# Retention and a rational feed-forward on one core: the order of work made by a queue model, attention taken ahead, weights split with two integer operations

## The chip, the cores and the metric

The kernel runs on one core of a Trainium2 chip. The time is device microseconds of one execution, from launch to end; the median of several is given. The engines are TensorE (PE, matrix products; PEld is its weight load), VectorE (DVE), ScalarE (ACT), GpSimd (POOL) and SyncE (SP, which issues all the transfers here). They run side by side, each through its own instructions in a fixed order, and wait for one another by semaphores.

## The reference

```python
def _attn_ref(q, k, v):                       # 8 batches, 8 heads, 576 positions, 64 wide
    scores = 1/sqrt(64) * q @ k.T
    gamma = 1 - 2.0 ** (-5 - arange(H))
    ret = scores * where(rel >= 0, gamma ** rel, 0)     # rel = query position - key position
    return ret @ v

def _moe_ref(x, w_in, w_out, a, b):           # x 4608 x 512, w_in 512 x 2048, w_out 2048 x 512
    h = x @ w_in
    P = a[0] + a[1]*h + a[2]*h**2 + a[3]*h**3
    Q = 1 + |b[0]|*|h| + |b[1]|*h**2
    return (P / (Q + 1e-6)) @ w_out
```

The attention's output, heads side by side, is x. The weights arrive as 64-bit floats.

## The kernel before, in words

**Attention** goes in 36 chunks of 128 positions (4.5 a batch, so a chunk can hold the end of one batch and the start of the next). A chunk n is loaded as two tiles, qk and kv. `scale_q` multiplies q by a table on POOL; `scale_v` scales v head by head, eight operations on ACT; `scores` is 16 small products into a tile `ps` in PSUM; `decay` has POOL zero two corners of a tile `s` and DVE multiply the scores by masks into it, in three operations; `outputs` forms the chunk's own part, the state's increment and the part that comes from the running state `S_sb`. `keep_hi` (ACT) and `keep_lo` (DVE) split the result into two fp32r tiles xhi and xlo, `add` (DVE) and `fade` (POOL) carry the state on.

**Feed-forward** goes in nine blocks b of 512 tokens, and in each over 16 slices f of 128 hidden columns. A pair (b, f) is a *step*; there are 144, numbered in the order in which they run: block 0's first eight slices, block 1, block 0's other eight, then blocks 2 to 8. `gemm1` forms h in one PSUM bank with 12 products (three for each of four parts: high by high, high by low, low by high), `gemm2` adds g times w_out into the accumulators `acc` with another 12. Between them h becomes g in eleven element operations on 128x512 tiles: p (ACT, then two on DVE), u = |h| (ACT), a line in u (ACT, called v), v (DVE), Ln and Exp (ACT) for 1/Q, then three on DVE, the first of which joins P and 1/Q and the other two of which are a correction step, then the high part of g (ACT) and its low part (POOL in the first 24 steps, DVE later).

**Weights**: 32 tiles (w_in and w_out, 16 each) of 64-bit words. `split_weight` takes the upper words through ACT (`c`), then three integer operations on DVE (a shift, a join with the top bits of the lower words, the sign), then a high part (ACT) and a low part (POOL), both fp32r. Chunks 2 to 5 are loaded into the slots of weight tiles that arrive later.

**Order.** It is written by hand. `BEFORE`, `FIRST`, `DENSE`, `REST` and `END` are lists of names; for each step `run` calls the functions named there in that order, and every operation keeps that order on its engine (`InOrder`). Five chunks run before step 0, chunk 5 to 7 in steps 1, 3 and 5, the others by `SCORES`. The products of w_out follow by `lag` steps:

```python
def lag(i):
    return 4 if NF // 2 <= i < first - 4 or i >= len(steps) - 8 else 3
```

PSUM has eight banks: two for h, four for acc (two tiles), two for ps. The loads stand in SP's queue as `load_unit` and `load_weight` are called.

Of the kernel before, what the change touches and what calls it, by code (L numbers as in the profile page):

```python
# [12 lines left out]
F32 = mybir.dt.float32  # L13
# [3 lines left out]
I64 = mybir.dt.int64  # L17
AF = mybir.ActivationFunctionType
# [14 lines left out]
BEFORE = "split1 start scale_q scale_v scores decay outputs split2 add fade keep_hi keep_lo split3 split0".split()  # L33
FIRST = (
    "split1 gemm1 outputs ffn_p split2 ffn_hi keep_hi ffn_lo gemm2 ffn_r scale_q split3 add fade keep_lo start ffn_p2"
    " scale_v scores decay split0 ffn_q ffn_v"
).split()
DENSE = (
    "gemm1 outputs keep_hi split1 add fade keep_lo ffn_p split2 split0 ffn_v scale_q ffn_hi ffn_r ffn_lo scale_v gemm2"
    " ffn_p2 scores decay split3 ffn_q"  # L40
).split()
REST = (
    "gemm1 ffn_p outputs keep_hi add fade keep_lo ffn_hi ffn_p2 ffn_lo scores decay scale_q scale_v ffn_v gemm2 ffn_r ffn_q"
).split()
END = "ffn_r ffn_hi gemm2 ffn_lo ffn_q".split()

STARTS_BEFORE = [0, 1, 1, 2, 2]
STARTS = [1, 1, 2, 1, 2] + [1] * 19

SCORES = [1, 3, 5, 23, 25, 27, 29, *range(2 * NF, (NB - 1) * NF, 4)]  # L50
WARM = [8, 3, 2]
LN_SHIFT = 60
# [12 lines left out]

@with_exitstack
def retention_ffn(ctx: ExitStack, tc: tile.TileContext, qkv, w_in, w_out, ab, masks, gq, gv, out):

# [15 lines left out]
    cnv = ctx.enter_context(tc.tile_pool(name="cnv", bufs=4))  # L84
# [36 lines left out]
    def warm(n):
        for _ in range(n):
            pe.matmul(unread[:, 0, 0:P], zeros, zeros, start=True, stop=True)

    warm(WARM[0])
    a0, a1, a2, a3 = (ab_sb[:, i : i + 1] for i in range(4))
    b0, b1 = absb[:, 0:1], absb[:, 1:2]
    lnb = const.tile([P, 2], F32, name="lnb")
    QC = float(np.float32(1.0) + np.float32(1e-6))
    dve.memset(lnb[:, 0:1], math.ldexp(QC, -LN_SHIFT))  # L130
    dve.memset(lnb[:, 1:2], -LN_SHIFT * math.log(2.0))


    bits = {}
    parts = {}

    def load_weight(k):

        bits[k] = wts.tile([P, DM], I64, tag=f"w{k[0]}_{k[1]}", name=f"bits{k[0]}_{k[1]}")
        nc.sync.dma_start(bits[k], (w_in, w_out)[k[0]][k[1]])  # L140

    def split_weight(k):


        nm = f"{k[0]}_{k[1]}"
        words = bits[k].bitcast(I32).rearrange("p (c w) -> p c w", w=2)
        low, high = words[:, :, 0], words[:, :, 1]
        c = cnv.tile([P, DM], I32, tag="c", name=f"c{nm}")
        cf = c.bitcast(F32)


        act.activation(cf, high.bitcast(F32), AF.Abs, scale=math.ldexp(1.0, -112))
        yield
        dve.tensor_scalar(c, c, 3, 1, ALU.logical_shift_left, ALU.bitwise_or)
        yield
        dve.scalar_tensor_tensor(c, low, 29, c, ALU.logical_shift_right, ALU.bitwise_or)
        yield
        dve.scalar_tensor_tensor(c, high, -0x80000000, c, ALU.bitwise_and, ALU.bitwise_or)
        yield
        w = wts.tile([P, 2, DM], F32R, tag=f"w{nm}", name=f"w{nm}")  # L160
        del bits[k]
        act.activation(w[:, 0, :], cf, AF.Copy)
        pool.tensor_tensor(w[:, 1, :], cf, w[:, 0, :].bitcast(F32), ALU.subtract)
        parts[k] = w


    xs = {}
    st_a = {}
    scr = {}
# [9 lines left out]
    def scale_q(n):  # L179

        q = raws[n][0][:, 0]
        pool.tensor_tensor(q, q, gq_sb, ALU.mult)

    def scale_v(n):

        v = raws[n][1][:, 1]
        for h in range(H):
            act.activation(v[:, h], v[:, h], AF.Copy, scale=gv_sb[:, h : h + 1])

    def scores(n):  # L190


        q, k = raws[n][0][:, 0], raws[n][0][:, 1]
        by_acc = n < NP and n % 3 < 2
        ps = (ps_acc if by_acc else ps_at).tile([P, 2, 512], F32, tag="acc" if by_acc else "at", name=f"ps{n}")
        for c in range(2):
            for e in range(2):
                for t in range(2):
                    for j in range(2):

                        g, r, i0 = 2 * c + e, slice(j * D, j * D + D), 64 * (t == e)
                        pe.matmul(
                            ps[t * D : (t + 1) * D, j, g * P + i0 : (g + 1) * P],
                            k[r, g, t * D : (t + 1) * D], q[r, g, i0:], start=True, stop=True,
                        )
        st_a[n] = ps

    def decay(n):

        ret = scr[n] = gp.tile([P, 2, 2, 2, P], F32, tag="g", name=f"s{n}")  # L210
        out_ = ret.rearrange("p j c e i -> p (j c) e i")
        in_ = st_a[n].rearrange("p j (c e i) -> p (j c) e i", c=2, e=2)
        r = [slice(P - D, P), slice(0, D)]
        for e in range(2):
            pool.memset(out_[r[1 - e], :, e, 0:D], 0.0)
        i0 = int(n % 9 == 4)
        m = mask_sb[:, 1 + i0 : 4 + i0 : 2].unsqueeze(1).broadcast_to([P, 4, 2, D])
        dve.tensor_tensor(out_[:, :, :, D:], in_[:, :, :, D:], m, ALU.mult)
        for e in range(2):
            m = mask_sb[r[e], 2 * e].unsqueeze(1).broadcast_to([D, 4, D])  # L220
            dve.tensor_tensor(out_[r[e], :, e, 0:D], in_[r[e], :, e, 0:D], m, ALU.mult)

    def parts_of(n):

        ps = st_a[n]
        return (
            ps[:, :, 0:256].rearrange("p j (c i) -> p j c i", c=2),
            ps[:, :, 256:384].rearrange("p e (c d) -> p c e d", c=2),  # L230
        )

    def outputs(n):


        u = n % 9
        o, ds = parts_of(n)
        ret = scr.pop(n)
        q = raws[n][0][:, 0]
        k, v = (raws[n][1][:, a] for a in range(2))  # L240
        for j in range(2):
            for c in range(2):
                for t in range(2):
# [14 lines left out]
        if u != 0:  # L258
# [297 lines left out]
```

## Time and profile before

| | |
|---|---|
| median of the runs | 984.15 us (983.35 to 984.31, three runs) |
| span of the profiled execution, first to last instruction | 979.8 us (its own time is given by its span alone) |
| busy: PE, DVE, ACT, POOL | 922.1, 841.8, 712.4, 167.8 us |
| mean granted clock of PE | 0.985 |
| bytes moved | 65.44 MB, 54.96 MB of them read |

The profile is one execution. The busy time of an engine is the union of its instructions; register, semaphore and transfer-issuing instructions are not counted. In the views by line nearly all instructions have line 63, that of the helper that records every operation, so the groups are told apart by what they write and read: `h<-xhi,w` is a product of gemm1, `acc<-w,g` one of gemm2, `ps<-...` one of attention, `c<-bits,c` a step of splitting a weight. A row of such a group gives its count, then its busy time in us, the mean ns of one, and the idle time of the engine just before, with what ended it.

### The profile page before, as it was taken

How to read it: one execution, taken by the hardware profiler on the slowest of the kernel's cores; microseconds unless marked ns; L12 is line 12 of the kernel's file. 1: busy time of each engine (PE TensorE's matmuls, PEld its weight loads, DVE VectorE, ACT ScalarE, POOL GpSimd, SP SyncE). 2: the span in 40 equal slices, each digit the busy share in tenths (PEclk: the TensorE clock that was granted, in tenths of full speed). 3: DMA queues.
4: the chain of work that ended last, by engine and by line, in shares of the span. 5: the costliest groups of instructions: out<-in, count | busy, mean ns of one | idle time of the engine just before them, and what ended most of it. 6: DMA issues, size and time to landing. Idle time of an engine off the chain costs nothing.

```text
span 979.8 us, 16128 instructions
## 1 busy us (share of the span) xinstructions
PE 922.1 (94%) x6234; PEld 745.3 (76%) x6234; DVE 841.8 (86%) x1261; ACT 712.4 (73%) x1274; POOL 167.8 (17%) x200
## 2 busy tenths in 40 slices
PE   6768877888999999999999999999999999999997
PEld 6547765656788888888888888888888888888886
DVE  4999989998788988888888888888888888888895
ACT  5487777776776777877787777777777777767775
POOL 3554434344011111101111111101111111100000
PEclk8799999999999999999999999999999999999999
DMA  9945000002212111210121112110211121001001
GB/s 348 407 165 210 7 0 1 1 1 87 86 44 86 44 44 43 87 65 22 44 87 43 44 44 86 44 65 23 87 44 43 44 87 44 2 1 43 1 0 44
DMA packets 20557, 65.44 MB, mean 67 GB/s; under 512 B 2304, under 2 KB 2432, under 8 KB 20480
## 3 DMA queue, kind: packets, MB, share of 16 engines
q1 hardware_dynamic: 20480, 64.41, 18.2%
q8 instruction: 49, 0.80, 0.3%
q14 instruction: 28, 0.23, 0.1%
HBM read 54.96 MB, written 9.44 MB: 66 GB/s over the span
## 4 chain that ended last, share of the span: by engine, by line
PE 75%; DVE 15%; ACT 4%; issue 3%; DMA 1%; POOL 0%; SPq 0%; ACTq 0%; POOLq 0%
PE acc L63 35%; PE h L63 33%; PE ps L63 8%; DVE c L63 7%; DVE p L63 5%; DVE v L63 2%; ACT c L63 1%; DMA kv<-in_qkv 1%; DVE s L63 1%; ACT kv L63 1%; ACT u L63 1%; DMA qk<-in_qkv 0%; ACT o L63 0%; ACT w L63 0%; ACT v L63 0%
## 5 line engine op out<-in xcount | busy, mean ns | idle before, releaser
L63 PE MATMUL acc<-w,g 128*128 128x512 f32 x1632 | 401.0, 394 | 7.5 <-ACT o L63 4.0
L63 PE MATMUL h<-xhi,w 128*128 128x512 f32 x1152 | 382.0, 393 | 16.3 <-DVE p L63 14.7
L63 PEld LDWEIGHTS acc<-w,g 128*128 128x128 f32 x1632 | 301.5, 188 | 78.6 <-ACT o L63 4.9
L63 PEld LDWEIGHTS h<-xhi,w 128*128 128x128 f32 x1152 | 217.2, 189 | 66.6 <-DVE p L63 18.9
L63 PE MATMUL h<-xlo,w 128*128 128x512 f32 x576 | 225.3, 391 | 0.2 <-DVE xlo L63 0.2
L63 ACT ACTIVATE p<-h,ab_sb 128x512 f32<-128x512 f32 x144 | 111.2, 772 | 106.5 <-PE h L63 106.4
L63 ACT ACTIVATE u<-h 128x512 f32<-128x512 f32 x144 | 85.7, 595 | 76.0 <-DVE v L63 74.6
L63 DVE SCALAR_TENSOR_TENSOR p<-p,ab_sb,u 128x512 f32<-128x512 f32 x144 | 107.8, 749 | 25.5 <-ACT u L63 22.1
L63 PEld LDWEIGHTS h<-xlo,w 128*128 128x128 f32 x576 | 108.7, 189 | 22.6 <-DVE xlo L63 0.5
L63 DVE TENSOR_TENSOR v<-v,u 128x512 f32<-128x512 f32 x144 | 99.6, 692 | 27.9 <-ACT v L63 27.7
L63 DVE TENSOR_TENSOR p<-p,h 128x512 f32<-128x512 f32 x144 | 98.8, 686 | 28.1 <-ACT u L63 27.7
L63 ACT ACTIVATE v<-u,absb 128x512 f32<-128x512 f32 x144 | 115.7, 803 | 0.4
L63 DVE SCALAR_TENSOR_TENSOR p<-p,ab_sb,h 128x512 f32<-128x512 f32 x144 | 107.0, 743 | 3.1
L63 ACT ACTIVATE u<-u,lnb 128x512 f32<-128x512 f32 x144 | 104.3, 724 | 4.7
L63 DVE SCALAR_TENSOR_TENSOR p<-v,p 128x512 f32<-128x512 f32 x144 | 99.7, 692 | 5.0
L63 ACT ACTIVATE u<-v,lnb 128x512 f32<-128x512 f32 x144 | 102.6, 712 | 0.2 <-DVE v L63 0.2
L63 DVE SCALAR_TENSOR_TENSOR v<-v,u 128x512 f32<-128x512 f32 x144 | 99.1, 688 | 0.0
L63 DVE TENSOR_TENSOR g<-p,g 128x512 fp32r<-128x512 f32 x112 | 91.4, 816 | 1.4 <-ACT g L63 1.4
L63 ACT ACTIVATE g<-p 128x512 fp32r<-128x512 f32 x136 | 85.7, 630 | 8.8 <-DVE p L63 3.3
L63 POOL TENSOR_TENSOR S_sb<-S_sb,gv_sb 128x256 f32<-128x256 f32 x32 | 20.3, 636 | 402.9 <-DVE S_sb L63 402.5
L63 ACT ACTIVATE kv<-kv,gv_sb 128x64 f32<-128x64 f32 x288 | 72.4, 337 | 9.9 <-DMA gv_sb<-in_gv 6.0
L63 DVE TENSOR_TENSOR s<-ps,mask_sb 64x256 f32<-64x256 f32 (+1 forms) x108 | 55.0, 509 | 10.3 <-DMA mask_sb<-in_masks 7.2
(36 smaller groups left out, 648.6 us busy)
## 6 DMA issues: line engine op xcount, KB each, us to landing
qk<-in_qkv SPq DMA_DIRECT2D x36, 512.0 KB, 4.8
kv<-in_qkv SPq DMA_DIRECT2D x36, 512.0 KB, 4.0
bits<-in_w_in SPq DMA_DIRECT2D x16, 512.0 KB, 10.2
bits<-in_w_out SPq DMA_DIRECT2D x16, 512.0 KB, 10.2
out<-o SPq DMA_DIRECT2D x16, 512.0 KB, 3.3
out<-o SPq DMA_DIRECT2D x4, 256.0 KB, 2.4
gq_sb<-in_gq SPq DMA_DIRECT2D x1, 256.0 KB, 2.8
mask_sb<-in_masks SPq DMA_DIRECT2D x1, 160.0 KB, 5.6
```

Source lines behind the costliest of these rows:

```text
L63: return lambda *a, **k: self.tc.keep_in_program_order(method(*a, **k))
```

## The change

A class `Plan` takes the place of the hand-written lists. Each operation, or group of operations, is a `Task` with an engine, a due time in units of steps, a cost in us, the tasks that it follows, and the buffers that it takes and gives back (`Ring`). `Plan.run` walks through time with a clock for each engine: of the tasks that could start within `SLACK` of the earliest it takes the one due first, emits its code, and advances. So the whole order, the loads on SP among it, is fixed while the program is built. Further:

- **Chunks 0 to 7** have due times from -30 to -16 and so stand ahead of step 0 (due 0) where they are ready. Their scores are eight full-width products instead of 16 smaller ones (chunk 8's too), their masking is one DVE operation without zeroing (two for chunk 4), and v is scaled by one operation on DVE. Chunks 8 to 11 are held until the gemm1 of step 21. Chunks 2 to 7 are loaded into later weights' slots.
- **h in four banks.** In steps 0 to 21, two of every four h tiles lie in the two banks of `ps`. There Ln and Exp write into h's own bank, from step 8 the line too, and so do the results of the two DVE operations in which 1/Q meets a second operand.
- **1/Q.** The factor of 2^-60 that stood in Ln's scale and Exp's bias is moved into b, so that Exp has no bias operand; the last scale on acc becomes -2^-60.
- **Weights.** The top bits of the lower words come from one ACT operation (`digit`, on 16-bit halves); a shift-and-or and the sign are the only DVE operations.
- In the first eight steps **v's multiplication** is on POOL.
- gemm2 of step i has due time i + 2.943, to the end.

```diff
-BEFORE = "split1 start scale_q scale_v scores decay outputs ...".split()
...
+EARLY = 8
+V_POOL = range(8)
+IN_BANK = 22
+WARM = 8
+AHEAD = -6
+REACH = 5.72
+UNITS = (19.78, 2.96)
+SV_DVE = 8
+LEAD = 2.47
+CNV = 3
+LOADS = 'w0 gq 0 mask w1 gv 1 w2 2 w3 3 w4 w5 ab 5 4 w7 6 w9 w8 w6 7 w10 w11'.split()
+LAG = {'PE': 0.25, 'ACT': 0.097, 'DVE': 0.217, 'POOL': 0.16, 'SP': 0}
+DUE = {'p_begin': 0.5, 'size': 0.775, 'p_mul': 0.7, ..., 'g_hi': 1.961, 'g_lo': 2.1, 'gemm2': 2.943, ...}
+SLACK = {'PE': 0.155, 'ACT': 0.2, 'DVE': 0.2, 'POOL': 0, 'SP': 0.028}
...
+    def run(self):
+        while left:
+            best = None
+            for e, queue in wait.items():
+                found = []
+                for t in queue:
+                    if e != "SP" and t.due > now + reach:
+                        continue
+                    ...
+                    s = max([clock[e], *ready, *(a.end - BACK[e] * (a.engine == e) for a in t.after)])
+                    if t.shared:
+                        s = max(s, port["POOL" if e == "DVE" else "DVE"])
+                    found.append((s, t.due, t))
+                ...
+                until = min(s for s, _, _ in found) + SLACK[e]
+                s, _, t = min((f for f in found if f[0] <= until), key=lambda f: f[1])
+                if best is None or s < best[0]:
+                    best = s, t
+            ...
+            t.emit()
...
 def split_weight / weight:
-        act.activation(cf, high.bitcast(F32), AF.Abs, scale=math.ldexp(1.0, -112))
-        dve.tensor_scalar(c, c, 3, 1, ALU.logical_shift_left, ALU.bitwise_or)
-        dve.scalar_tensor_tensor(c, low, 29, c, ALU.logical_shift_right, ALU.bitwise_or)
-        dve.scalar_tensor_tensor(c, high, -0x80000000, c, ALU.bitwise_and, ALU.bitwise_or)
+            act.activation(c_[0].bitcast(F32), words()[1].bitcast(F32), AF.Abs, scale=math.ldexp(1.0, -112))
+            act.activation(c_[1], words()[2], AF.Copy, scale=15 * 2.0**-17)
+            dve.scalar_tensor_tensor(c_[0], c_[0], 3, c_[1], ALU.logical_shift_left, ALU.bitwise_or)
+            dve.scalar_tensor_tensor(c_[0], words()[1], -0x80000000, c_[0], ALU.bitwise_and, ALU.bitwise_or)
+        d = min(s - LEAD, AHEAD + order)
...
 def scale_v:
+            if n < SV_DVE:
+                dve.tensor_tensor(v, v, gv_sb[:, 0:H].unsqueeze(2).broadcast_to([P, H, D]), ALU.mult)
+                return
...
 def gemm1:
+            if wide:                                   # i < 22 and i % 4 >= 2
+                if i % 4 == 2:
+                    pair[0] = ps_at.tile([P, 2, 512], F32, tag="at", name=f"h{i}")
+                h = pair[0][:, i % 4 - 2]
...
-        act.activation(u, v, AF.Ln, bias=lnb[:, 0:1], scale=math.ldexp(1.0, -LN_SHIFT))
-        act.activation(u, u, AF.Exp, bias=lnb[:, 1:2], scale=-1.0)
+            act.activation(e["r"], e["v"], AF.Ln, bias=qc)         # r: h's bank in steps 0 to 21, else u
+            act.activation(r, r, AF.Exp, scale=-1.0)
...
+        v_pool = i in V_POOL
+            (pool if v_pool else dve).tensor_tensor(e["v"], e["line"], e["u"], ALU.mult)
...
+        t1 = add("PE", i, 2.72, gemm1, after, takes)
+        tl = add("POOL" if by_pool else "DVE", i + DUE["g_lo"], 1.21 if by_pool else 0.6, g_lo, [th], [], [("p", key)], shared=True)
+            "PE", i + DUE["gemm2"], 2.72, gemm2, a, ...
...
+    for n in range(EARLY):
+        attention(n, -30 + 2 * n, 2, got[n], consts, prev, [])
+        if i == 2 * NF:
+            hold = [products[(*steps[IN_BANK - 1][:2], 0)]]
+            for n in range(EARLY, NU):
+                d = UNITS[0] + UNITS[1] * (n % 4) if n < 12 else 16 * (n // 4 - 1) + 1 + 4 * (n % 4)
+                attention(n, d, 1, load_unit(n, d - 3), consts, prev, hold)
```

More of the change, by code (lines that the diff above doesn't have):

```diff
@@ L31, with begin_of @@
 NP = 4
[L33 to L52, printed above, removed]
+EARLY = 8
[8 more added lines that the diff above has]
+CNV = 3
+CNT = 1
+SHIFT = 60
+LOADS = 'w0 gq 0 mask w1 gv 1 w2 2 w3 3 w4 w5 ab 5 4 w7 6 w9 w8 w6 7 w10 w11'.split()
+def begin_of(name):
+    return LOADS.index(str(name)) - 1000 if str(name) in LOADS else 1000
+LAG = {'PE': 0.25, 'ACT': 0.097, 'DVE': 0.217, 'POOL': 0.16, 'SP': 0}
+BACK = {'PE': 0.25, 'ACT': 0.109, 'DVE': 0.06, 'POOL': 0.075, 'SP': 0.0}
+DUE = {'p_begin': 0.5, 'size': 0.775, 'p_mul': 0.7, 'p_mul2': 0.722, 'v_line': 0.814, 'v_mul': 1.1, 'log': 1.3, 'exp': 1.5, 'quot': 1.6, 'check': 1.65, 'better': 0.706, 'g_hi': 1.961, 'g_lo': 2.1, 'gemm2': 2.943, 'begin': 0.0, 'digit': 0.05, 'join': 0.128, 'sign': 0.2, 'high_part': 1.252, 'low_part': 0.8, 'scale_q': -0.354, 'scale_v': -0.5, 'scores': 0.405, 'decay': 0.2, 'outputs': 0.822, 'cross': 0.51, 'keep_hi': 1.353, 'keep_lo': 0.898, 'grow': 0.6, 'fade': 0.7}
+SLACK = {'PE': 0.155, 'ACT': 0.2, 'DVE': 0.2, 'POOL': 0, 'SP': 0.028}
 class InOrder:
@@ L114, in retention_ffn @@
     absb = const.tile([P, 2], F32, name="absb")
+    qc = const.tile([P, 1], F32, name="qc")
     S_sb = const.tile([P, NPAIR, D], F32, name="S_sb")
+    state = S_sb.rearrange("p (c e) d -> p c e d", e=2)
+    a0, a1, a2, a3 = (ab_sb[:, i : i + 1] for i in range(4))
+    b0, b1 = absb[:, 0:1], absb[:, 1:2]
+    QC = math.ldexp(float(np.float32(1.0) + np.float32(1e-6)), -SHIFT)
+    BACK_TO = -math.ldexp(1.0, -SHIFT)
     zeros = S_sb.rearrange("p g d -> p (g d)")[:, 0:P]
@@ L119, in retention_ffn @@
     unread = ps_at.tile([P, 2, 512], F32, tag="at", name="unread")
[L121 to L131, printed above, removed]
@@ L167, in retention_ffn, with load @@
-    xs = {}
-    st_a = {}
-    scr = {}
+    for _ in range(WARM):
+        pe.matmul(unread[:, 0, 0:P], zeros, zeros, start=True, stop=True)
+    dve.memset(qc, QC)
+    def load(due, kb, dst, src, **k):
+        return add("SP", due, kb / 390.0, lambda: sp.dma_start(dst, src), **k)
+    half = NF // 2
+    runs = [(0, 0, half), (1, 0, NF), (0, half, NF)] + [(b, 0, NF) for b in range(2, NB)]
+    steps = [(b, f, f == r0, f == r1 - 1) for b, r0, r1 in runs for f in range(r0, r1)]
+    at = {s[:2]: i for i, s in enumerate(steps)}
@@ L177, in x_of, with x_part @@
         return xs[b]
[L179 to L196, printed above, removed]
-            for e in range(2):
-                for t in range(2):
-                    for j in range(2):
-                        g, r, i0 = 2 * c + e, slice(j * D, j * D + D), 64 * (t == e)
+    def x_part(x, un):
+        return x[:, :, (un % 4) * P : (un % 4 + 1) * P].rearrange("p (j c) i -> p j c i", j=2)
@@ L359, in ffn_hi, with at_ @@
-    def ffn_hi(b, f):
-        g = gs[b, f] = place(b, f)
-        act.activation(g[:, 0, :], els[b, f][2], AF.Copy)
-    def ffn_lo(b, f, by_pool):
-        p = els.pop((b, f))[2]
-        g = gs[b, f]
-        if by_pool:
-            pool.tensor_tensor(g[:, 1, :], p, g[:, 0, :].bitcast(F32), ALU.subtract)
-        else:
-            dve.tensor_tensor(g[:, 1, :], p, g[:, 0, :].bitcast(F32), ALU.subtract)
-    def gemm2(b, f, first, last):
-        if first:
-            accs[b] = [ps_acc.tile([P, 2, DM], F32, tag="acc", name=f"acc{b}_{f}_{t}") for t in range(2)]
-        g = gs.pop((b, f))
-        w = parts[1, f]
-        for t in range(4):
-            ts = slice(t * P, (t + 1) * P)
-            acc = accs[b][t // 2][:, t % 2, :]
-            for k, (i, j) in enumerate(((0, 0), (0, 1), (1, 0))):
-                pe.matmul(acc, g[:, i, ts], w[:, j, :], start=(first and k == 0), stop=(last and k == 2))
-        if not last:
+        def at_(x):
+            return d + gap * x
@@ new lines, in attention @@
+        tq = add("POOL", at_(DUE["scale_q"]), 1.21, scale_q, [got[0], consts["gq"]], shared=True)
+        sv = n < SV_DVE
+        tv = add("DVE" if sv else "ACT", at_(DUE["scale_v"]), 0.6 if sv else 1.9, scale_v, [got[1], consts["gv"]], shared=sv)
+        ts = add("PE", at_(DUE["scores"]), 0.9, scores, [tq, *hold], [(ring, key)])
+        if dense:
+            tm = add("DVE", at_(DUE["decay"]), 1.13, decay, [ts, consts["mask"]], [("g", key)])
+        else:
+            tz = add("POOL", at_(-0.1), 0.6, clear, [ts], [("g", key)], shared=True)
+            tm = add("DVE", at_(DUE["decay"]), 1.02, decay, [ts, tz, consts["mask"]])
@@ new lines, in attention @@
+        to = add("PE", at_(DUE["outputs"]), 1.5, outputs, [tm, tv], [], [("g", key)])
+        done = [to]
+        if u:
+            tx = add("PE", at_(DUE["cross"]), 0.7, cross, [to, prev["fade"]])
+            done = [tx]
+        if not 2 <= n < EARLY:
+            for t, nm in ((done[0], "qk"), (to, "kv")):
+                t.gives.append((nm, n))
+                plan.rings[nm].left[n] = 1, 0.0
+        gives = [(ring, key)]
+        th = add("ACT", at_(DUE["keep_hi"]), 0.5, keep_hi, done, [("xp", b)] if n % 4 == 0 else [], gives)
@@ L461, in retention_ffn @@
-    nc.sync.dma_start(gq_sb, gq)
-    load_unit(0)
-    nc.sync.dma_start(gv_sb, gv)
-    nc.sync.dma_start(mask_sb, masks)
-    for n in range(1, 6):
-        load_unit(n)
-        load_weights(1 if n < 3 else 2)
-    nc.sync.dma_start(ab_sb, ab)
-    scale_q(0)
-    scale_v(0)
-    for n in range(NP + 1):
-        before(n)
-    act.activation(absb, ab_sb[:, 4:6], AF.Abs)
-    nxt, due, done = NP + 1, [(NP, 0)], 0
-    def products(i):
-        nonlocal done
-        while done < len(steps) and i - done >= lag(i):
-            gemm2(*steps[done])
-            done += 1
@@ L483, in retention_ffn @@
[L483 to L505 removed]
+                    ck = f"o{t}{j}"
@@ new lines, in retention_ffn @@
+    consts = {"gq": load(begin_of("gq"), 256, gq_sb, gq)}
+    got = {n: load_unit(n, begin_of(n)) for n in range(EARLY)}
+    consts["gv"] = load(begin_of("gv"), 6, gv_sb, gv)
+    consts["mask"] = load(begin_of("mask"), 160, mask_sb, masks)
+    t_ab = load(begin_of("ab"), 3, ab_sb, ab)
+    t_ab = add("ACT", -1, 0.2, lambda: act.activation(absb, ab_sb[:, 4:6], AF.Abs, scale=math.ldexp(1.0, -SHIFT)), [t_ab])
+    prev = {}
+    for n in range(EARLY):
+        attention(n, -30 + 2 * n, 2, got[n], consts, prev, [])
@@ new lines, in retention_ffn, with emit @@
+    for k, (s, w, f) in enumerate(need):
+        def emit(w=w, f=f):
+            bits[w, f] = wts.tile([P, DM], I64, tag=f"w{w}_{f}", name=f"bits{w}_{f}")
+            sp.dma_start(bits[w, f], (w_in, w_out)[w][f])
+        n = f - (NF - EARLY)
+        hold = [last_of[n]] if 2 <= n < EARLY else []
+        weight(k, s, w, f, add("SP", min(begin_of(f"w{k}"), s - 8), 524 / 390.0, emit, hold))
+    for i, (b, f, begins, ends) in enumerate(steps):
+        if i == 2 * NF:
[3 more added lines that the diff above has]
+                attention(n, d, 1, load_unit(n, d - 3), consts, prev, hold)
+        feed_forward(i, b, f, begins, ends)
```

594 lines of the change are left out of this document (380 added, 214 removed).

## The prediction

> **What bounds the kernel now.** I read the page first: busy shares and slices.
>
> ```profile
> span 979.8 us, 16128 instructions
> PE 922.1 (94%) x6234; PEld 745.3 (76%) x6234; DVE 841.8 (86%) x1261; ACT 712.4 (73%) x1274; POOL 167.8 (17%) x200
> PE   6768877888999999999999999999999999999997
> DVE  4999989998788988888888888888888888888895
> PEclk8799999999999999999999999999999999999999
> ```
>
> PE is full from the eleventh slice on. Before that it is not, and VectorE (DVE) is. So there are stages with different limits. I cut the span where PE starts certain products: 37.85 is the first product with w_in (step 0), 102.82 that of step 8, 216.40 that of step 24, 252.08 that of step 28. The view by windows; columns are length, busy time of PE, PEld, DVE, ACT, POOL, granted clock, DMA share, GB/s:
>
> ```profile
> 0.00:37.85 37.85, 22.78 (x363) 20.31 (x363) 22.01 (x38) 18.13 (x54) 14.52 (x25) 0.82 0.96 368
> 37.85:102.82 64.97, 53.85 (x444) 42.15 (x445) 62.46 (x89) 46.91 (x92) 33.25 (x32) 0.92 0.56 214
> 102.82:216.40 113.58, 93.12 (x417) 71.25 (x415) 102.73 (x141) 83.53 (x134) 46.99 (x33) 1.00 0.00 1
> 216.40:252.08 35.68, 29.70 (x231) 23.19 (x225) 29.72 (x46) 27.74 (x57) 12.09 (x14) 0.95 0.26 90
> 252.08:979.80 727.72, 722.68 (x4794) 588.42 (x4788) 624.90 (x951) 536.11 (x942) 60.97 (x98) 1.00 0.14 47
> ```
>
> Call them A to E. In E, PE is idle for 727.72 - 722.68 = 5.0 us, the last eviction and store. What VectorE or ScalarE (ACT) saves there is worth nothing, since PE's products are unchanged. From A to D, PE is idle for 252.08 - 199.45 = 52.6 us: that is nearly all there is to win.
>
> In C, DVE is busy for 102.73 of 113.58 us. The chain of waits repeats one pattern there, of which I show two starts, then one product group, then the end:
>
> ```profile
> 105.88 1.07 DVE c L63
> 113.09 1.07 DVE c L63
> ...
> 374.90 2.72 PE h L63 x12
> ...
> 961.18 13.61 PE acc L63 x60
> ```
>
> A step of C takes 113.09 - 105.88 = 7.21 us, against 2 x 2.72 = 5.44 us of products. DVE's share in it that splits weights, with POOL's beside it, from the groups of 105 to 190 us kept apart by shape (busy, mean ns):
>
> ```profile
> L63 DVE SCALAR_TENSOR_TENSOR c<-bits,c 128x512 int32<-128x512 int32 x23 | 21.2, 924 | 0.0
> L63 POOL TENSOR_TENSOR g<-p,g 128x512 fp32r<-128x512 f32 x12 | 18.7, 1561 | 36.8 <-issue 33.8 <-ACT g L63 3.0
> L63 POOL TENSOR_TENSOR w<-c,w 128x512 fp32r<-128x512 f32 x12 | 15.6, 1296 | 16.3 <-ACT w L63 16.3
> L63 DVE TENSOR_SCALAR c<-c 128x512 int32<-128x512 int32 x12 | 12.8, 1069 | 7.9 <-ACT c L63 7.9
> L63 ACT ACTIVATE c<-bits 128x512 f32<-128x512 f32 x12 | 7.8, 649 | 0.0
> ```
>
> and the same two DVE operations, with the masking of a chunk, in the timeline where POOL is quiet or nearly so:
>
> ```profile
> 17.99 0.42 DVE L63 TENSOR_SCALAR c<-c 128x512 int32<-128x512 int32 x1
> ...
> 20.08 1.55 DVE L63 TENSOR_TENSOR s<-ps,mask_sb 128x512 f32<-128x512 f32 x3
> 21.55 0.67 DVE L63 SCALAR_TENSOR_TENSOR c<-bits,c 128x512 int32<-128x512 int32 x1
> ```
>
> The three integer operations take 1.069 + 2 x 0.924 = 2.92 us a weight, and 0.42 + 2 x 0.67 = 1.76 us undisturbed. The other 1.16 us is waiting inside the instruction, beside POOL's two subtractions.
>
> **The change part by part.** The span is summed as A+B, C, D, E. The rows that price the rest: the element operations over the whole run,
>
> ```profile
> L63 ACT ACTIVATE p<-h,ab_sb 128x512 f32<-128x512 f32 x144 | 111.2, 772 | 106.5 <-PE h L63 106.4
> L63 ACT ACTIVATE u<-h 128x512 f32<-128x512 f32 x144 | 85.7, 595 | 76.0 <-DVE v L63 74.6
> L63 DVE SCALAR_TENSOR_TENSOR p<-p,ab_sb,u 128x512 f32<-128x512 f32 x144 | 107.8, 749 | 25.5 <-ACT u L63 22.1
> L63 DVE TENSOR_TENSOR v<-v,u 128x512 f32<-128x512 f32 x144 | 99.6, 692 | 27.9 <-ACT v L63 27.7
> L63 ACT ACTIVATE v<-u,absb 128x512 f32<-128x512 f32 x144 | 115.7, 803 | 0.4
> L63 ACT ACTIVATE u<-u,lnb 128x512 f32<-128x512 f32 x144 | 104.3, 724 | 4.7
> L63 DVE SCALAR_TENSOR_TENSOR p<-v,p 128x512 f32<-128x512 f32 x144 | 99.7, 692 | 5.0
> L63 ACT ACTIVATE u<-v,lnb 128x512 f32<-128x512 f32 x144 | 102.6, 712 | 0.2 <-DVE v L63 0.2
> L63 DVE SCALAR_TENSOR_TENSOR v<-v,u 128x512 f32<-128x512 f32 x144 | 99.1, 688 | 0.0
> L63 DVE TENSOR_TENSOR g<-p,g 128x512 fp32r<-128x512 f32 x112 | 91.4, 816 | 1.4 <-ACT g L63 1.4
> L63 ACT ACTIVATE g<-p 128x512 fp32r<-128x512 f32 x136 | 85.7, 630 | 8.8 <-DVE p L63 3.3
> ```
>
> the unread products and the 1024-wide eviction from the same view,
>
> ```profile
> L63 PE MATMUL unread<-S_sb 128*128 128x128 f32 x26 | 5.5, 382 | 1.1 <-DVE S_sb L63 1.1
> L63 DVE SCALAR_TENSOR_TENSOR o<-acc,o 128x1024 f32<-128x1024 f32 x2 | 2.3, 1208 | 0.0
> ```
>
> and single pieces from the timeline:
>
> ```profile
> 1.06 3.78 PE L63 MATMUL unread<-S_sb 128*128 128x128 f32 x16 [1.06 <-DVE S_sb L63]
> 6.99 0.90 PE L63 MATMUL ps<-qk 64*64 64x64 f32 x32 [2.15 <-POOL qk L63]
> ...
> 16.21 1.09 PE L63 MATMUL ps<-s,kv 128*64 128x128 f32 x16
> ...
> 223.54 2.42 PE L63 MATMUL ps<-s,kv 128*64 128x128 f32 x16 [4.13 <-POOL s L63]
> ...
> 504.68 2.01 ACT L63 ACTIVATE kv<-kv,gv_sb 128x64 f32<-128x64 f32 x8
> ```
>
> *C, two integer operations.* TENSOR_SCALAR and one SCALAR_TENSOR_TENSOR go: 16 x (1.069 + 0.924) = 31.9 us off DVE's 102.73, leaving 70.8. DVE drops below PE's 16 x 5.44 = 87.0. What is late next is ACT: the new digit operation reads strided words and writes 512 integers, as c<-bits does, so 16 x 0.649 = +10.4 us; Exp loses its bias operand, and the nearest row without one is u<-h, so 16 x (0.724 - 0.595) = -2.1 us. ACT comes to 83.53 + 10.4 - 2.1 = 91.8 us, above PE's 87.0. I take 91.8, a gain of 21.8. Ends: 87.0 (ACT's splitting runs ahead of the steps, as REACH allows) and 105.6, that is 6.6 us a step: from 7.21 only the undisturbed 0.42 + 0.67 go, and some 0.5 comes back as waits in the operations that stay.
>
> *1/Q in place.* Up to step 21 Ln, Exp and mostly the line write the h bank. No operation of before writes PSUM from ACT or DVE, so I price them at their SBUF rows, with 0.1 us each way on some three a step (22 x 3 x 0.1 = 6.6 us) as bounds, inside C's ends. h is then freed only after the last DVE operation, not after the second; four banks instead of two pay for that.
> The Trainium skill, "ScalarE: Activation LUTs", section "Step-by-step: what each stage is for", says that ScalarE writes PSUM faster than SBUF. By that rule C would come near 87.0 and the whole to 939. No row here shows such a write.
>
> *A and B, eight chunks first.* DVE there is 84.47 us; some 14 weights lose 1.99 each (-27.9), the masking becomes one instruction of about 1.21 (the 1024-wide row) for 1.55 (8 x -0.34 = -2.7), six v multiplications go to POOL (-4.2), and scaling of v comes over at about 0.69 (+5.5): 55. ACT: 65.0 + 14 x 0.649 - 8 x 2.01 = 58. Either is well under the stage, so PE sets it. Its work after the first scores is 76.63, less 3.78 unread before them, less about 1.75 unread among them (the view shows 26 in 5.5 us, and 8 stay), plus the dense scores: eight full-width products two at a time are shaped like the 1.09 us row instead of the 0.90 one, 8 x 0.19 = 1.5. That is 72.6. The first scores start at 6.99, and later by the w0 tile now loaded ahead of q (524 KB at 368 GB/s = 1.4 us). So A+B is at least 8.4 + 72.6 = 81.0 instead of 102.82. Chunk 7 must also land: eight units of 1.05 MB, ten weights of 0.52 and the tables make 14.0 MB, 38 us at 368 GB/s. Products of steps 0 to 2 can fill PE until then but not wholly, and the state goes from chunk to chunk over PE, DVE and POOL. I take 5 us of idle: 86, a gain of 16.8. Ends 81 and 96. What is queued behind: all loads are on SP in one order, and the weights from f = 10 on wait there for chunks 2 to 7; the first is split near step 12, far behind. POOL carries scaling of q, fading, low parts, g's low part and v: about 3 x 1.3 a step, under 5.44.
>
> *D.* Chunk 8 waits 4.13 us there for the zeroing on POOL, which is now dropped for it and placed early for others. PE's busy time is 29.70; I take 31.7 (gain 4.0; ends 29.7 and 35.7). The hold of chunks 8 to 11 until step 21's product costs nothing if four chunks fit before step 32.
>
> *E.* Same products, DVE and ACT below PE, so 0 from the steady part. At the end, before keeps four products of 2.72 between the last h and its own product (13.61 us with it). A due time of 2.943 leaves two or three (5.4 to 8.2), while the chain of one tile, p, u, v, the multiplication, Ln, Exp, three on p and v, g twice, sums from the rows to 7.87. I add 2 (ends 0 and 5).
>
> Sum: 86 + 91.8 + 31.7 = 209.5 for 252.08, -42.6; E +2: span 939.2. The median of the runs, 984.15, lies 4.35 above the profiled span, which I keep: 943.6, so **944**.
>
> **Rivals.** *PE alone binds:* A+B 81, C 87.0, D 29.7, E +0: -54.4, 930. For it: all three other engines have room by the sums. Against: ACT at 91.8 in C, and clock 0.82 in A.
>
> *The port keeps the pace:* the 1.16 us of waits do not leave with the operations, because POOL now has up to three long operations a step beside DVE's two-input ones. C at 6.6 a step gains 8.0, A+B gains 8, D 3, E loses 2: -17, 967. For it: 0.42 became 1.069 beside POOL. Against: quot, check and better now have one operand in PSUM, and one weight brings two operations beside POOL instead of three.
> The Trainium skill, "SBUF — State Buffer", section "SBUF: two separate sides", calls the port pair of DVE and GpSimd an exclusive lock, taken by DVE operations with two SBUF inputs. The stretched rows agree with that; by it the three operations in the bank escape, which speaks for my case, and v on POOL speaks against.
>
> *Slower: the fixed order starves PE in E.* Today gemm2(i-3) follows gemm1(i), so six groups, 16.3 us, lie between a tile's h and its use. A due of i + 2.943 puts it ahead of gemm1(i + 3): four groups, 10.9 us. The chain needs 7.87 plus queueing on a DVE that is busy for 624.90 of 727.72. The planner counts 0.6 for g's low part, and the row says 0.816. If it is optimistic, PE waits each step in an order that cannot adapt. With 116 steps left, 0.35 us a step (40.5 us) cancels the gain; 0.5 makes it 58 us, 1002.
>
> *No change:* the written order comes to the same as before and the start stays bound by loads: 984.
>
> **How the numbers follow.** My case (936 to 958) 0.54; PE alone 0.17; port 0.17; slower 0.10; no change 0.02. Faster by over 0.2% (about what a measurement here can tell) is 0.54 + 0.17 + 0.17 = 0.88. Below 926 I leave 0.03 of PE alone, above 968 0.05 of the port's case and the 0.12 of the last two: 926 to 968.
>
> **What would show it.** In the profile after: step 8's product near 86, step 24's near 178, PE in the slices 3 to 8 at nine tenths; c rows of DVE 64 instead of 96; ACT above 95% in C with PE's waits there on ACT; E unchanged at 2.72 a group; a gap of some 2 us before the last twelve products. It is wrong if E shows PE gaps on g, if C's period stays above 6.3, or if A stays at 38 with DMA waits.

## The result, and the profile after

| | before | after |
|---|---|---|
| median of the runs | 983.75 us (981.99 to 984.31, four) | 944.73 us (943.63 to 947.71, four) |
| span of the profiled execution | 979.8 us | 941.8 us (its run took 943.63) |
| PE busy; span less PE busy | 922.1; 57.7 us | 913.5; 28.3 us |

The ratio is 0.9617 (0.9594 to 0.964): 39.0 us faster by the medians, 38.0 by the two profiled spans. The page of after, busy shares and slices:

```profile
span 941.8 us, 15566 instructions
PE 913.5 (97%) x6080; PEld 740.8 (79%) x6080; DVE 788.7 (84%) x1211; ACT 702.6 (75%) x1242; POOL 171.4 (18%) x190
PE   5998999899999999999999999999999999999997
DVE  4998788989798888898888888888888888888885
PEclk9999999999999999999999999999999999999999
```

PE's row is near nine tenths from the second slice on, where before it was at 6 to 8 for ten slices. The row of the granted clock stays at nine tenths, where before it began with 8 and 7. Of the 38.0 us of span, 57.7 - 28.3 = 29.4 are PE's idle time; the other 8.6 are busy time, for nearly the same products (6080 for 6234) at a higher mean clock (0.996 for 0.985). The windows of after, cut at the same products as before (steps 0, 8, 24, 28):

```profile
0.00:34.14 34.14, 22.25 (x288) 19.92 (x288) 19.88 (x29) 13.44 (x23) 15.58 (x19) 0.95 0.96 369
34.14:80.20 46.06, 44.09 (x371) 35.53 (x369) 43.05 (x65) 38.59 (x67) 30.50 (x25) 1.00 0.83 330
80.20:187.34 107.14, 98.40 (x445) 76.83 (x446) 91.14 (x134) 95.59 (x175) 51.72 (x40) 0.98 0.03 11
187.34:213.40 26.06, 25.96 (x260) 20.66 (x258) 22.18 (x35) 21.99 (x45) 12.36 (x15) 1.00 0.32 112
213.40:941.80 728.40, 722.80 (x4726) 587.87 (x4720) 612.46 (x952) 533.01 (x938) 61.23 (x94) 1.00 0.14 46
```

A+B is 80.20 us (102.82 before), C 107.14 (113.58), D 26.06 (35.68), E 728.40 (727.72). By the order of PE's instructions the cuts hold not quite the same work: at step 8 after has four products of w_out behind it, before five; C of after holds the whole of chunk 8 and one product more, D one product less. At step 28 they agree again (one product of w_out less, one chunk more). So the cut at step 28, 213.40 for 252.08, is the one to trust: all of the gain lies ahead of it. In C neither DVE (91.14 of 107.14) nor ACT (95.59) is full; PE is busy for 98.40. What PE waits for from 30 to 255 us (us in total, number of waits, longest), first the two largest of eight kinds in before, 44.3 us in all, then all of after:

```profile
PE ps L63 <- POOL s L63: 14.8, 4, 4.5
PE h L63 <- DVE p L63: 14.7, 10, 1.5
```

```profile
PE acc L67 <- POOL g L67: 3.8, 6, 0.9
PE h L67 <- DVE p L67: 2.8, 3, 1.3
PE h L67 <- ACT u L67: 2.1, 3, 0.9
PE acc L67 <- ACT g L67: 1.7, 2, 0.9
PE ps L67 <- DVE p L67: 0.3, 1, 0.3
```

10.7 us in fifteen waits, each under 1.4 us and on different engines: late hand-overs, no engine that is full. Gone are the 14.8 us in four waits of attention's products for POOL's operation on `s`, the zeroing; the prediction had counted one of them, the 4.13 us in D. The weight operations and those that write h's bank, over the whole run:

```profile
L67 DVE SCALAR_TENSOR_TENSOR c<-bits,c 128x512 int32<-128x512 int32 x32 | 26.0, 819 | 0.2
L67 DVE SCALAR_TENSOR_TENSOR c<-c,t 128x512 int32<-128x512 int32 x32 | 25.5, 796 | 4.6 <-ACT t L67 4.6
...
L67 ACT ACTIVATE h<-v,qc 128x512 f32<-128x512 f32 x22 | 15.2, 689 | 2.3 <-DVE p L67 1.9 <-DVE v L67 0.4
L67 DVE SCALAR_TENSOR_TENSOR h<-v,h 128x512 f32<-128x512 f32 x22 | 15.1, 687 | 0.0
...
L67 ACT ACTIVATE h<-h 128x512 f32<-128x512 f32 x22 | 12.9, 584 | 2.9 <-DVE p L67 2.4
...
L67 ACT ACTIVATE h<-u,absb 128x512 f32<-128x512 f32 x14 | 11.0, 784 | 4.0 <-DVE p L67 3.9
```

A weight now costs DVE 0.82 + 0.80 = 1.62 us for 2.92, and the waiting inside the instructions has gone from 1.16 to about 0.28 us a weight (0.67 undisturbed for each operation). The operation `h<-v,h`, with an operand in the bank, takes 687 ns, as its SBUF form did before (688).

### The profile page after: what moved, and what is told of

It is laid out like the page before. It is cut to its first block, busy times and chain, and to the rows that moved or that the text cites. A ratio compares the mean times of both kernels' runs of the same rounds, so it can differ in the third digit from the quotient of the medians.

```text
span 941.8 us, 15566 instructions
## 1 busy us (share of the span) xinstructions
PE 913.5 (97%) x6080; PEld 740.8 (79%) x6080; DVE 788.7 (84%) x1211; ACT 702.6 (75%) x1242; POOL 171.4 (18%) x190
## 4 chain that ended last, share of the span: by engine, by line
PE 84%; DVE 6%; ACT 5%; issue 2%; POOL 1%; DMA 1%; SPq 0%; DVEq 0%; ACTq 0%; POOLq 0%
PE h L67 38%; PE acc L67 36%; PE ps L67 9%; DVE p L67 3%; ACT h L67 2%; ACT p L67 1%; DVE c L67 1%; ACT u L67 1%; DMA gv_sb<-in_gv 1%; ACT g L67 1%; DVE s L67 1%; DVE h L67 0%; POOL w L67 0%; DVE v L67 0%; ACT c L67 0%
## 5 line engine op out<-in xcount | busy, mean ns | idle before, releaser
L67 DVE SCALAR_TENSOR_TENSOR p<-p,ab_sb,h 128x512 f32<-128x512 f32 x166 | 123.4, 744 | 7.8 <-ACT h L67 4.5
L67 ACT ACTIVATE u<-v,qc 128x512 f32<-128x512 f32 x122 | 87.9, 720 | 46.9 <-DVE v L67 46.5
L67 DVE SCALAR_TENSOR_TENSOR p<-p,ab_sb,u 128x512 f32<-128x512 f32 x122 | 91.9, 753 | 31.9 <-ACT u L67 31.8
L67 ACT ACTIVATE v<-u,absb 128x512 f32<-128x512 f32 x130 | 105.9, 814 | 3.4
L67 DVE TENSOR_TENSOR v<-v,u 128x512 f32<-128x512 f32 x122 | 89.7, 735 | 0.0
L67 DVE SCALAR_TENSOR_TENSOR p<-v,p 128x512 f32<-128x512 f32 x122 | 84.4, 692 | 4.2
L67 DVE SCALAR_TENSOR_TENSOR v<-v,u 128x512 f32<-128x512 f32 x122 | 84.3, 691 | 0.0
L67 ACT ACTIVATE u<-u 128x512 f32<-128x512 f32 x122 | 76.5, 627 | 2.1
L67 POOL TENSOR_TENSOR qk<-qk,gq_sb 128x512 f32<-128x512 f32 x36 | 48.3, 1341 | 122.8 <-DMA qk<-in_qkv 122.7
L67 ACT ACTIVATE kv<-kv,gv_sb 128x64 f32<-128x64 f32 x224 | 56.3, 335 | 0.0
```

The source lines that it names most:

```text
L67: return lambda *a, **k: self.tc.keep_in_program_order(method(*a, **k))
```

## The experiments

The theory was the prediction's: PE was starved by a DVE that splitting and waits beside POOL filled; the rival, that order and chunks make the gain. A second question was what sets the pace of C after. Each time is the median; each ratio is against runs of the kernel before on the same chip.

| kernel | us | ratio, interval |
|---|---|---|
| e1_three_ops | 973.1 | 0.9904 (0.9876 to 0.9932) |
| e2_two_banks | 974.2 | 0.9909 (0.9883 to 0.9935) |
| e3_five_first | 974.1 | 0.9913 (0.9880 to 0.9946) |
| e4_order_alone | 983.4 | 1.0005 (0.9989 to 1.0020) |
| e5_before_two_ops | 973.2 | 0.9906 (0.9883 to 0.9930) |
| e6_digit_twice | 974.5 | 0.9918 (0.9896 to 0.9939) |
| e7_no_digit | 960.0 | 0.9760 (0.9733 to 0.9788) |
| e8_v_on_dve | 953.5 | 0.9706 (0.9683 to 0.9730) |
| f1_cost_digit | 954.6 | 0.9706 (0.9690 to 0.9722) |
| f2_lead | 956.8 | 0.9728 (0.9710 to 0.9745) |
| f3_same_order_no_digit | 942.0 | 0.9581 (0.9560 to 0.9602) |
| f4_same_order_three_ops | 960.5 | 0.9767 (0.9752 to 0.9781) |

**One part undone, the order made anew (e1, e2, e3).**

```diff
 e1: -            act.activation(c_[1], words()[2], AF.Copy, scale=15 * 2.0**-17)
     +            dve.tensor_scalar(c_[0], c_[0], 3, 1, ALU.logical_shift_left, ALU.bitwise_or)
     +            dve.scalar_tensor_tensor(c_[0], words()[0], 29, c_[0], ALU.logical_shift_right, ALU.bitwise_or)
 e2: -IN_BANK = 22
     +IN_BANK = 0
 e3: -EARLY = 8
     +EARLY = 5
     +    for n in range(EARLY, 8):
     +        attention(n, 1 + 2 * (n - EARLY), 1, load_unit(n, -4 + 2 * (n - EARLY)), consts, prev, [])
```

> The changed kernel with three integer operations on DVE a weight, as before, and no digit operation on ACT; the order is made anew by the same planner. Theory (PE was starved by a DVE that the weight splitting and its waits beside POOL filled, and the relief of DVE is a main part of the gain): DVE has 32 x 0.42 to 1.07 us more, steps 8 to 23 get longer, 953 us (949 to 962). Rival (order and chunks made the gain; with them the third operation finds room, and ACT, which was the next bound, is relieved by 0.65 a weight): 944 us or less (938 to 947).

> The changed kernel with h in two banks in all steps and Ln, Exp, the line and the two DVE results in SBUF tiles, as before; chunks 8 to 11 still held until the gemm1 of step 21. Theory: quot, check and better, with both operands in SBUF again, wait beside POOL's operations, 1 us a step in some 20 steps on a DVE with 15% to spare: 952 us (947 to 960). Rival (the bank only gives other storage, and DVE has room): 945 (943 to 947).

> The changed kernel with five chunks ahead of step 0 instead of eight, chunks 5 to 7 due in steps 1, 3 and 5 and loaded after earlier chunks, not into weights' slots. Theory (PE's idle time in the first 80 us is filled by whatever is ready; attention ahead removes the waits for state and scores among the products): 951 us (946 to 960), with PE idle time back between 35 and 90 us. Rival (a planner that fits chunks in between does as well): 945 (942 to 948).

All three came to 973 to 974 us, outside the ranges of both sides. That is some 29 us lost each, three quarters of the whole gain. Three parts cannot each be worth three quarters. Either they need one another, or something that all three kernels share costs time.

**All parts undone but the planner (e4), and one part alone in the old order (e5).**

```diff
 e4: e1 and e2 and e3 together, and
     -V_POOL = range(8)
     +V_POOL = range(0)
     -SV_DVE = 8
     +SV_DVE = 0
     -        dense = n < EARLY + 1
     +        dense = n < 0
 e5, in the kernel before:
     -        dve.tensor_scalar(c, c, 3, 1, ALU.logical_shift_left, ALU.bitwise_or)
     +        act.activation(low, half_words, AF.Copy, scale=15 * 2.0**-17)
              yield
     -        dve.scalar_tensor_tensor(c, low, 29, c, ALU.logical_shift_right, ALU.bitwise_or)
     +        dve.scalar_tensor_tensor(c, c, 3, low, ALU.logical_shift_left, ALU.bitwise_or)
```

> All parts of the change but the planner undone together: three integer operations, two banks and SBUF tiles, five chunks first, quadrant scores with zeroing on POOL, v scaled on ACT, v's multiplication on DVE. What is left is the planner's order and loads, and Exp without a bias. Theory (the parts, above all DVE's relief, make most of the gain): 972 us (962 to 982). Rival (the order alone makes most of it): 955 or less.

> The kernel before, its hand-written order kept, with the digit taken on ACT (in place in the weight's words, at the place in the lists where the shift stood) and two integer operations on DVE. Theory (DVE is the bound of steps 8 to 23, 7.21 us each): a step loses the shift's 1.07, some 16 to 24 us in all, 963 us (957 to 972). Rival (the fixed order ties DVE and ACT in a loop, and the operation only moves from one to the other): 980 (974 to 986).

The planner alone, with the constants of the changed kernel, is no faster than the lists (1.0005); the theory's 962 to 982 was too hopeful. These constants were chosen for the changed kernel, and an order chosen for the old parts was not tried. e4 zeroes `s` on POOL again, and no wait of PE from 30 to 255 us is put down to it; one of 7.4 us for DVE's operation on `s` stands there instead, and 27.3 us in eleven waits for `p` from DVE.

In e5 the digit operation alone gives 10 us, which lies between the theory's 957 to 972 and the rival's 974 to 986. Its steps in C, in the chain of waits, in the groups of 105 to 190 us and in the window of C:

```profile
106.78 0.68 DVE c L64
...
113.45 0.69 DVE c L64
```

```profile
L64 DVE SCALAR_TENSOR_TENSOR v<-v,u 128x512 f32<-128x512 f32 x13 | 23.2, 1785 | 0.0
L64 POOL TENSOR_TENSOR w<-c,w 128x512 fp32r<-128x512 f32 x12 | 20.5, 1706 | 16.3 <-ACT w L64 16.3
...
L64 DVE SCALAR_TENSOR_TENSOR c<-bits,c 128x512 int32<-128x512 int32 x13 | 15.4, 1188 | 0.0
...
L64 DVE SCALAR_TENSOR_TENSOR c<-c,bits 128x512 int32<-128x512 int32 x13 | 8.9, 684 | 0.0
```

```profile
101.27:205.68 104.41, 92.23 (x418) 71.52 (x416) 103.56 (x124) 90.79 (x148) 52.95 (x33) 1.00 0.00 1
```

A step takes 113.45 - 106.78 = 6.67 us for 7.21. The shift of 1.07 us went, but `check` (`v<-v,u`, the first operation of the correction step), 0.68 us before, is now 1.79: it is the one that meets POOL's low part (1.71 us). So in the fixed order the wait found another DVE operation with two SBUF operands, as the prediction's port rival had it, and at its pace of 6.6. The Trainium skill, "SBUF — State Buffer", section "SBUF: two separate sides", says that such an operation and a GpSimd one lock each other out for the whole instruction; this trace agrees, 1.79 being 0.68 plus 1.11 of the 1.71 us of POOL's low part.

DVE's busy time in C has not fallen: it is 103.56 of 104.41 us, for 102.73 of 113.58 before. What e5 saves in C is idle time of DVE, 0.85 us for 10.85. In before most of that was the shift's wait for `c` from ACT, 7.9 us in the row that the prediction shows.

What frees the changed kernel of the waits inside the instructions can be read from e2, which has an order of the planner and two integer operations, but no bank operands. Rows of DVE from 105 to 190 us:

```profile
L67 DVE SCALAR_TENSOR_TENSOR p<-p,ab_sb,u 128x512 f32<-128x512 f32 x13 | 13.1, 1010 | 2.8 <-ACT u L67 2.7
L67 DVE SCALAR_TENSOR_TENSOR c<-bits,c 128x512 int32<-128x512 int32 x11 | 12.5, 1132 | 0.2
...
L67 DVE TENSOR_TENSOR v<-v,u 128x512 f32<-128x512 f32 x12 | 10.4, 865 | 0.0
...
L67 DVE SCALAR_TENSOR_TENSOR c<-c,t 128x512 int32<-128x512 int32 x11 | 8.6, 782 | 0.0
```

The waits are back. Against 0.74, 0.67, 0.68 and 0.67 us undisturbed, these four rows are 12.0 us too long in 85 us; the integer rows of before are 13.6 too long there, those of after 3.8. Counted in the same way over all of DVE's 128x512 operations there, the four kernels without bank operands (before, e2, e4, e5) have 13 to 20 us of such waiting, and the ten with them, in eight different orders, 3 to 7. So it is the bank operands, not the order and not the missing operation, that free DVE of most of it.

**ACT's load doubled and taken away, and v on DVE, orders made anew (e6, e7, e8).**

```diff
 e6: +            act.activation(c_[1], words()[2], AF.Copy, scale=15 * 2.0**-17)
     -        t = add("ACT", d + DUE["digit"], 0.55, digit, [t], [("t", k)])
     +        t = add("ACT", d + DUE["digit"], 1.1, digit, [t], [("t", k)])
 e7: +    dve.memset(no_digit, 0)
     -            dve.scalar_tensor_tensor(c_[0], c_[0], 3, c_[1], ALU.logical_shift_left, ALU.bitwise_or)
     +            dve.scalar_tensor_tensor(c_[0], c_[0], 3, no_digit, ALU.logical_shift_left, ALU.bitwise_or)
 e8: -V_POOL = range(8)
     +V_POOL = range(0)
```

> The changed kernel with the digit operation on ACT done twice, its cost doubled in the planner. If ACT sets the pace of steps 8 to 23, as the prediction had it: some 16 to 20 more operations of 0.56 there, +9 to +11 us, 954 (952 to 957). If ACT only has to keep up with PE and has 10% to spare: +2 to +5, 948 (946 to 950).

> The changed kernel without the digit operation: the join takes a tile of zeros instead, so the weights lose the top three bits of their lower words; DVE's operations are as many as in the changed kernel. If ACT sets the pace of steps 8 to 23: -7 to -9 us, 936. If the hand-overs in the order and PE's own work do: -1 to -3, 943 (941 to 944).

> The changed kernel with v's multiplication on DVE in the first eight steps too, the line then written to h's bank. Theory: the first 80 us are set by PE and the loads, DVE has room there: +-1, 944.5 (943 to 947). Rival (DVE is still near full there): +4 to +6, 949.

All three came out slower than either side expected. e7 is the telling one: with less work on ACT and the same on DVE the kernel is 15 us slower. That points to the new order, which the next runs test. All of these kernels are alike after some 255 us, and differ ahead of it. So these three, and e1 to e3, measure a part and a new order together.

**The order alone, then a part alone in the kept order (f1 to f4).** The first two alter one number of the planner and no operation. In the other two the planner reckons as in the changed kernel, and what is emitted in its places differs.

```diff
 f1: -        t = add("ACT", d + DUE["digit"], 0.55, digit, [t], [("t", k)])
     +        t = add("ACT", d + DUE["digit"], 0.57, digit, [t], [("t", k)])
 f2: -LEAD = 2.47
     +LEAD = 2.5
 f3: -            act.activation(c_[1], words()[2], AF.Copy, scale=15 * 2.0**-17)
     +            c_[1] = no_digit
 f4: -            act.activation(c_[1], words()[2], AF.Copy, scale=15 * 2.0**-17)
     +            return
     -            dve.scalar_tensor_tensor(c_[0], c_[0], 3, c_[1], ALU.logical_shift_left, ALU.bitwise_or)
     +            dve.tensor_scalar(c_[0], c_[0], 3, 1, ALU.logical_shift_left, ALU.bitwise_or)
     +            dve.scalar_tensor_tensor(c_[0], words()[0], 29, c_[0], ALU.logical_shift_right, ALU.bitwise_or)
```

> The changed kernel with one number of the planner altered: the digit operation is reckoned at 0.57 us instead of 0.55. Every operation is the same; only the order is, in some 180 of 4367 places from about step 5 on. Theory (the eight kernels before this one differ by what their newly made order does in the first 250 us, more than by the work that was taken out or put back): 956 us (949 to 968). Rival (the work decides, and orders of the same planner are as good as one another): 945 (943 to 948).

> The same with another number: weights are due 2.50 steps ahead of need instead of 2.47. Theory, of the order: 955 us (948 to 968). Rival, of the work: 945 (943 to 948).

> The digit operation left out, the join taking a tile of zeros (the weights lose the top three bits of their lower words), but the order kept as the changed kernel has it: the planner still reckons with the operation and emits nothing in its place. If ACT's work sets the pace of steps 8 to 23, as the prediction had it: 936 to 939 us. If the order of hand-overs does, and PE's own work: 943 to 945. If the loss of 15 us in the newly planned kernel without the digit came from the work: 960.

> Three integer operations on DVE and no digit on ACT, in the changed kernel's order: the shift stands directly ahead of the join, the digit's place on ACT is left empty. Its loss is the price of the third operation on DVE alone. Theory (DVE has 15% to spare in steps 8 to 23, the shift takes 0.42 to 1.07 us a weight of it, and part of that delays the tiles that PE waits for): 953 us (948 to 960). Rival (the loss of 28 us with a new order was the operation's own): 968 to 974.

f1 and f2: the same operations in another order of the same planner cost 10 and 12 us, inside the theory's ranges. The waits of PE in f1, from 30 to 255 us:

```profile
PE acc L67 <- POOL g L67: 4.0, 5, 1.2
PE acc L67 <- ACT g L67: 3.1, 3, 1.8
PE ps L67 <- DVE p L67: 2.8, 1, 2.8
PE h L67 <- ACT p L67: 2.7, 1, 2.7
PE h L67 <- DVE p L67: 1.9, 3, 0.9
PE ps L67 <- DVE s L67: 1.3, 1, 1.3
```

It is the same kind of wait as in after, but longer, and single ones reach 2.8 us; all nine kinds, of which six are shown, make 17.4 us for 10.7. Step 28 begins at 229.03 instead of 213.40, with two more products of w_out (5.4 us) done by then. PE's busy time grows too, from 913.5 to 917.7 us for the same products, at a mean granted clock of 0.991 for 0.996.

The view by windows, cut at the same products as that of after: C of f3, then C, D and E of f4:

```profile
81.15:186.86 105.71, 98.27 (x445) 76.58 (x444) 91.82 (x134) 87.25 (x159) 51.78 (x40) 0.98 0.04 11
```

```profile
86.25:203.16 116.91, 101.50 (x445) 78.66 (x446) 103.96 (x153) 88.28 (x159) 52.27 (x40) 0.96 0.03 10
203.16:229.05 25.89, 25.89 (x260) 20.63 (x258) 20.40 (x34) 21.52 (x42) 12.32 (x13) 1.00 0.33 113
229.05:957.50 728.45, 722.79 (x4726) 587.97 (x4720) 611.57 (x951) 533.24 (x938) 61.28 (x96) 1.00 0.14 46
```

f3: ACT is busy for 87.25 instead of 95.59 us, 8.3 less, and C is 1.1 shorter (1.4 by the window, whose first cut in f3 lies one product, 0.33 us, late). The time, 942.0, lies between the two forecasts (936 to 939 and 943 to 945), nearer the second. The intervals of the ratios overlap (0.956 to 0.960, 0.959 to 0.964). So ACT's work does not set the pace of C. And e7's 960 was its order: the same work in the kept order is at 942, 18 us apart.

f4, half a us above the 948 to 960 that was expected: a third DVE operation a weight in the digit's place costs 960.53 - 944.73 = 15.8 us, and 18.5 against f3, which has no digit either. The 15.8 are 6.0 in A+B (86.25 for 80.20), 9.8 in C (116.91 for 107.14), nothing in D and E. DVE's busy time in C grows by 12.8 us to 103.96 of 116.91, 89%, as in before (90%). The tiles that PE needs come later, and PE's own products take longer, 101.50 us for 98.40, at a granted clock of 0.96 for 0.98. PE's waits for p from DVE rise to 8.0 us:

```profile
PE h L67 <- DVE p L67: 8.0, 4, 3.5
PE h L67 <- ACT u L67: 4.6, 4, 2.4
```

So of e1's 28 us, about 16 are the operation and 12 the new order, if the two add. What two banks (e2) or five chunks (e3) cost in the kept order was not tried; if their new orders cost what the measured ones did, 10 to 18 us, 11 to 19 us of each are left. That is an estimate. e8's 9 us is no more than a new order costs, so v's place has no price that these runs show. Of the theory and the rival neither holds alone: the relief of DVE by one operation a weight is worth 16 to 18 us in the kept order, and an order that fits is worth 10 to 18.

## Why the prediction was right, point by point

The time was 944.0 forecast, 944.73 measured. The main steps hold: PE's idle time ahead of step 28 was most of what could be won, E gives nothing, and 29.4 of the 38.0 us of span are PE's idle time going from 57.7 to 28.3 us. That the sum came so near is luck. A+B, C and D all lie outside the ends that the prediction gave them (81 and 96, 87.0 and 105.6, 29.7 and 35.7): they are off by -5.8, +15.3 and -5.6 us, E by -1.3 and the way from span to time by -2.5, and these cancel. Term by term:

- **A+B: 86 forecast, 80.20 measured.** It is even under the floor of 81.0. The first scores start at 8.47, as reckoned (8.4), and the idle time after them is 9.2 us, more than the 5 assumed. But PE's work after them is 62.6 us (66.34 less 3.78 unread) instead of 72.6. One product of w_out (2.72) has moved into C. The remaining 7.3 I put down to the granted clock, which went from 0.82 and 0.92 to 0.95 and 1.00 and which I had kept. Why the clock rose is not shown: PE idled less in both stages, but in before's C it had 1.00 while PE was idle for 20.5 of 113.58 us.
- **C: 91.8 forecast, 107.14 measured.** About 4.4 of it is work moved in (a product at 2.72, some 1.7 of chunk 8). The other 11 us are the failed step "What is late next is ACT". ACT's work was sized about rightly (91.8 forecast; 95.59 measured, of which 2.0 are chunk 8's scaling), but it is not the pace; f3 took 8.3 us of it away for 1.1. What paces C is PE at 98.40 of 107.14, with waits at hand-overs from DVE and ACT, which are 85 and 89% busy, and from POOL. The sum over the fullest engine is a floor here, and the waits add 9% to PE's busy time. The prediction had named a period above 6.3 us in C as a sign that it is wrong, and the period is 107.14 / 16 = 6.70, or 6.42 without the work moved in: for this step of the prediction the sign holds.
- **D: 31.7 forecast, 26.06 measured.** The idle time of 5.98 us has gone but for 0.10, the 4.13 us wait for the zeroing with it. PE is busy for 25.96 instead of 29.70; 2.72 of the difference are one product of w_out that now runs in E.
- **A to D together: 209.5 forecast, 213.40 measured**, 3.9 too hopeful.
- **E: +2 forecast, +0.7 measured.** The end is as forecast: three products (the first two rows below, 12 instructions each) lie between the last h and its own, where before had four, and PE waits 0.84 us ahead of its own:

```profile
924.01 5.60 PE L67 MATMUL acc<-w,spare 128*128 128x512 f32 x24
929.69 3.29 PE L67 MATMUL acc<-w,g 128*128 128x512 f32 x12
933.82 3.29 PE L67 MATMUL acc<-w,g 128*128 128x512 f32 x12 [0.84 <-ACT g L67]
```

- **From span to time: 4.35 kept, 1.83 measured** (943.63 - 941.8). I had set the span of one run against the median of others. Runs of before whose own spans are on record lie 1.7 to 1.9 above them (984.07 for 982.3). This hid the 2.6 us by which the span was too low.

The rivals. *PE alone* (930) failed by the same hand-overs. *The port* (967): by its length alone, 6.70 us a step, C would fit this rival's 6.6. Its mechanism is refuted in the changed kernel, where the stretch fell to 0.28 us a weight and no other DVE operation in C is stretched, and confirmed in the old order by e5, at 6.67 us a step. The escape needs the bank operands: the missing operation alone does not give it (e5), nor does an order of the planner (e2). One reading of the prediction falls short there: the shift, which reads one tile only, stretched most (0.42 to 1.069 us), so two SBUF inputs do not explain every stretched row. *The fixed order starves PE in E*: the planner does put w_out's product ahead of the next h in 98 of 144 steps, as feared, but PE is busy for 722.80 of 728.40 there and the chain shows groups of 2.72 back to back; the chain of one tile fits. In the first 255 us the mechanism is real at a smaller price, 10 and 12 us in f1 and f2. *No change* is nearly what e4 gave, where the parts are missing.

What the prediction did not see is that its parts do not add. The planner alone gives 0, the digit alone 10, both with all other parts 39; and an order from the same planner with one number off by 0.02 us is 10 us worse. In the kept order the runs price one part only, the third DVE operation, at 16 to 18 of the 39 us. Eight chunks ahead, the bank operands, the masking without zeroing and the scaling of v have no price of their own in it, so which of them makes the rest stays open.

## What to carry to other kernels

Where one engine is full later and starved earlier, count its idle time in the early part first: as long as its work and its clock stay the same, that is the most that any relief of the other engines can give (here 8.6 of the 38.0 us came from shorter busy time besides). Compare a forecast term by term: a sum can be right while its terms are not. An experiment that undoes one part of a kernel whose order is planned also makes a new order, and this one moved the time by 10 to 18 us; keep the order and change what is emitted, or alter a number of the planner alone to see how much an order is worth. Removing an instruction that waits on a shared resource may only move the wait to the next instruction, so look for it in the durations of those that stay.

## What the runs showed of the hardware

ACT operations that write PSUM were shorter than the same ones writing SBUF: Ln 689 ns against 720, Exp 584 against 627, the line 784 against 814, from the groups of after (the first of each pair is shown above, the second is its row in SBUF tiles):

```profile
L67 ACT ACTIVATE v<-u,absb 128x512 f32<-128x512 f32 x130 | 105.9, 814 | 3.4
...
L67 ACT ACTIVATE u<-v,qc 128x512 f32<-128x512 f32 x122 | 87.9, 720 | 46.9 <-DVE v L67 46.5
...
L67 ACT ACTIVATE u<-u 128x512 f32<-128x512 f32 x122 | 76.5, 627 | 2.1
```

The two kinds of row come from different steps; in C, where three lines still go to SBUF, those take 804 ns. For Exp the source is in PSUM as well. The Trainium skill, "ScalarE: Activation LUTs", section "Step-by-step: what each stage is for", says that PSUM is the faster target; the trace agrees, by 30 to 43 ns in 512 elements, within the 0.1 us that the prediction allowed. Exp without a bias operand is 627 ns in SBUF, 97 less than the 724 with one (the prediction took 129 from a row of another function). The same page of the Trainium skill, section "What ACT_TABLE_LOAD costs", gives about 93 ns for such an operand, and the trace agrees.
